# Reordering the first batch of a fused attention and maxout kernel: early scores, a weight transpose, and one load's place

## The chip, the cores and the metric

The kernel runs on one core of one Trainium2 chip. The metric is the device time of one execution in microseconds (us), lower is better. The core has a matrix engine (PE, with its weight loads as a row of their own, PEld), a vector engine (DVE), a scalar engine (ACT), GpSimd (POOL) and SyncE (SP), each with its own instruction stream, and 16 DMA engines that serve the loads and stores which SP, ACT and POOL issue.

## The reference

Block-causal attention over 8 batches, 8 heads, 576 tokens and head size 64 (blocks of 64 tokens), followed by a maxout layer on the 4608 tokens of width 512:

```python
scores = scale * np.matmul(q, k.transpose(0, 1, 3, 2))
mask = (pos // 64)[:, None] >= (pos // 64)[None, :]
scores = np.where(mask, scores, -1000000000.0)
attn = exp(scores - max) / (sum + 1e-09)
x = (attn @ v).transpose(0, 2, 1, 3).reshape(4608, 512)
h1 = x @ w1            # w1, w2: 512 x 1024
h2 = x @ w2
g = np.maximum(h1, h2)
return g @ w_out       # w_out: 1024 x 512
```

## The kernel before

The maxout is rewritten: max(h1, h2) = h2 + max(x (w1 - w2), 0). So the kernel forms `d_sb` = w1 - w2 (`diff_w`, DVE), the product `m_sb` = w2 w_out (from transposes of w2, `bT_unit`, and matmuls, `m_unit`), then for each span of tokens `g` = max(x d, 0) (`h_unit`) and the output rows y = x m + g w_out (`y_unit`). Inputs come as float32 and are cast to bf16; sums are float32.

Attention works on pairs of heads, p = 0 to 31, four pairs to a batch; two pairs are a group g, whose q and k come in one load each (`load_qk`, 576 KB, issued on SP). With `gated=True` POOL first writes one column of the load's tile with a memset (L119), and SP's issue waits for that memset; where the memset stands in POOL's stream is where the load is let go. `cast` makes bf16 of it (DVE, ACT or POOL), `transposes` turns it on PE into two PSUM tiles, whose copies to `qT` and `kT` are left to `copy_out`. V of a batch comes in five chunks (`load_v`, issued by POOL, which casts in flight). The weights are also loaded by POOL: w1 in `load_w`, w2 into a part of `xT` that is not in use yet, w_out in `load_wo`.

The scores of a pair are matmuls into one of two PSUM tiles (`ps_s`), exp on ACT writes them to `aT`, and small memsets (`mask`) clear what the block mask excludes. In batch 0 each pair has four bursts: `burst_p` covers the first 256 tokens, and `burst_q1`, `burst_q2`, `burst_q3` the rest. Later pairs have three tiles (`tile_0` to `tile_2`). `av(p, ts)` multiplies with V and scales by the sums on DVE; `x_out` transposes the result on PE and copies it to `xT`, in later batches a DMA does so.

Everything but the scores' tiles shares four rotating PSUM tiles (`ps_m`): a new one waits for the readers of the one four before it. For the transposes of group 1 in the first stage these are all four, and what comes next needs the copies of `cq` and `ck` in turn. `LOW` and `HIGH` split these copies by token, so that `burst_p` needs LOW alone.

The order of the first batch is written out by hand, line by line, and each engine takes its instructions in that order. `warm_up(n)` puts n matmuls of zeros (128x512) into PE's stream. `fill(n)` takes work worth n matmuls of 512 columns from a planned list of units (`h_unit`, `bT_unit`, `m_unit`, `y_unit`), first in the list whose tokens are there. A unit started is finished before the next. From the third group on a loop places scores, exps, products and fills; `pool_work(s)` there puts loads, casts and V chunks in POOL's stream, and is called by hand for s = 4 and s = 5.

The planned list starts with two h units, which need the first 256 tokens of x, then the transposes of w2's first piece, which need no token:

```python
for f in range(NFF):
    h(i, f)
    if i == 0 and f % 2:
        units.append((bT_unit(f // 2), 0, 0.25, 2 * NDM))
```

Of the kernel before, what the change touches and what calls it, by code (L numbers as in the profile page):

```python
# [14 lines left out]
def kernel(  # L15
# [10 lines left out]
    nc = tc.nc  # L26
# [33 lines left out]
    def a_col(p, c, t):  # L60
        if p >= HP:
            return CB[c] + t * P
        late = t * P >= QCUT
        return t * P + {
            0: 384 - QCUT if late else 0, 1: 704 - QCUT if late else 256 - P,
            2: 1024 - QCUT, 3: 1408 - 3 * P, 4: 1344 - 4 * P,
        }[c]
# [42 lines left out]
    dve, pool, act = nc.vector.tensor_copy, nc.gpsimd.tensor_copy, nc.scalar.copy  # L110

    def load_qk(g, queues, gated=False):
        b, u = divmod(g, GPB)
        for nm, src, queue in (("q", q, queues[0]), ("k", k, queues[1])):
            if queue is None:
                continue
            raws[nm, g] = t = raw.tile([P, 2, RPP * D], FP32, name=f"{nm}raw")
            if gated:
                nc.gpsimd.memset(t[:, 0, :1], 0.0)  # L119
            queue.dma_start(  # L120
                out=t[:],
                in_=src[b, 4 * u:4 * u + 4].rearrange(
                    "(s h) (p t) d -> (h p) s (t d)", h=2, t=RPP),
            )

    def cast(nm, g, parts):
        t = raws[nm, g].rearrange("p s (t d) -> p t s d", d=D)
        if (nm, g) not in qk_n:
            qk_n[nm, g] = qkn.tile([P, RPP, 2, D], BF16, name=f"{nm}n")
        n = qk_n[nm, g]  # L130
        for copy, j0, j1 in parts:
            copy(out=n[:, j0:j1], in_=t[:, j0:j1])  # L132

    def load_v(b, c):
        rows = min(P, S - c * P)
        nc.gpsimd.dma_start(  # L136
            out=vv_r[b % NV][P - rows:, c, :, :D],
            in_=v[b, :, c * P:c * P + rows, :].rearrange("h p d -> p h d"),
        )
# [20 lines left out]
    def diff_w(j):  # L160
        fs = slice(j * WB, (j + 1) * WB)
        nc.vector.tensor_sub(d_sb[:, :, fs], w1_raw[j][:], w2_sb[j])
# [8 lines left out]
    dve, pool, act = nc.vector.tensor_copy, nc.gpsimd.tensor_copy, nc.scalar.copy  # L171
    SP, ACT = nc.sync, nc.scalar
# [149 lines left out]
    def fill(n):  # L322
        while n > 0:
            if not current:
                k = next((k for k, t in enumerate(todo) if t[2] <= done_tokens[0]), None)
                if k is None:
                    return max(0, n)
                current.append(todo.pop(k))
            t = current[0]
            next(t[1])  # L330
            n -= t[3]
            t[0] -= 1
            if not t[0]:
                current.pop()
        return 0


    def warm_up(n):
        pw = ps_m.tile([P, SPAN], FP32, name="ps_w", tag="m")
        for _ in range(n):  # L340
            nc.tensor.matmul(pw[:], zeros[:, :P], zeros[:], start=True, stop=True)
# [57 lines left out]
    def mask(p, a0, eng=None):  # L399
        (eng or nc.gpsimd).memset(aT_r[p % NA][BLK:, :, a0:a0 + BLK], 0.0)  # L400

    def burst(p, parts, a0):
        u = ps_s.tile([P, 2, 512], FP32, name="ps_s", tag="s")
        w = 0
        for c, q0, n in parts:
            scores(p, u, w, c, q0, n)
            w += n
        exp(p, u, w, a0)

    def burst_p(p):  # L410
        burst(p, ((0, 0, QCUT), (1, P, QCUT - P)), 0)

    def burst_q1(p):
        burst(p, ((0, QCUT, 320), (1, QCUT, 192)), 384)

    def burst_q2(p):
        burst(p, ((1, 448, P), (2, QCUT, 320), (4, 512, BLK)), 896)

    def burst_q3(p):
        burst(p, ((3, 384, 192),), 1408)  # L420

    def masks_p(p, eng=None):
        for a in (0, 256):
            mask(p, a, eng)
# [7 lines left out]
    def tile_0(p):  # L432
        u = ps_s.tile([P, 2, 512], FP32, name="ps_s", tag="s")
        scores(p, u, 0, 0, 0, 512)
        return lambda: (exp(p, u, 512, 0), mask(p, 0))
# [27 lines left out]
    def av(p, ts):  # L463
        b, hp = divmod(p, HP)
        vv = vv_r[b % NV]
        a = aT_r[p % NA]
        n = len(ts)
        h0 = hp // 2 * 4 + hp % 2
        if p % 2 == 0 and ts[0] == 0:
            xps[p // 2] = xpool.tile([P, 2, NCH, 2, D], BF16, name="xp")  # L470
        xp = xps[p // 2]
        po = ps_m.tile([P, n, 2, D + 1], FP32, name="ps_o", tag="m")
        n_mm = 2 * sum(t + 1 for t in ts)
        mm = 0
        for gi, t in enumerate(ts):
            for hh in range(2):
                for c in range(t + 1):
                    a0 = a_col(p, c, t)
                    nc.tensor.matmul(  # L479
                        po[:, gi, hh, :], a[:, hh, a0:a0 + P], vv[:, c, h0 + 2 * hh, :],  # L480
                        start=(mm == 0), stop=(mm == n_mm - 1),
                    )
                    mm += 1
        rec = small.tile([P, 3, 2, 1], FP32, name="rec")
        nc.vector.reciprocal(rec[:, :n, :, 0], po[:, :, :, D])  # L485
        nc.vector.tensor_mul(  # L486
            xp[:, :, ts[0]:ts[0] + n, p % 2].rearrange("q s t d -> q t s d"), po[:, :, :, :D],
            rec[:, :n].to_broadcast([P, n, 2, D]),
        )

    def x_by_dma(g):
        return BY_DMA <= g < NG - 1
# [10 lines left out]
    def x_out(g, t0=0, t1=NCH, copies=(dve, dve)):  # L503
        b, u = divmod(g, GPB)
        if x_by_dma(g):
            if u == GPB - 1:
                done_tokens[0] = (b + 1) * S
            return
        xp = xps[g]
        n = t1 - t0  # L510
        n_odd = min(t1, NCH - 1) - t0
        pe = ps_m.tile([P, 2, n, BLK], BF16, name="ps_xe", tag="m")
        po = ps_m.tile([P, 2, n_odd, BLK], BF16, name="ps_xo", tag="m")
        for s in range(2):
            for t in range(t0, t1):
                src = xp[:, s, t].rearrange("p a d -> p (a d)")
                nc.tensor.transpose(pe[:, s, t - t0, :], src[:BLK], ident[:BLK, :BLK])
                if t < NCH - 1:
                    nc.tensor.transpose(po[:, s, t - t0, :], src[BLK:], ident[BLK:, BLK:])
        dst = xT[:, 2 * u:2 * u + 2, b * S + t0 * P:b * S + t1 * P].rearrange(  # L520
            "p s (t h w) -> p s t h w", h=2, w=BLK)
        copies[0](out=dst[:, :, :, 0], in_=pe[:])
        copies[1](out=dst[:, :, :n_odd, 1], in_=po[:])
        if u == GPB - 1:
            done_tokens[0] = min(b * S + t1 * P, (b + 1) * S)
# [14 lines left out]

    def pool_work(s):
        g, i = divmod(s, 2)
        if s == 4:
            load_qk(4, (SP, SP), gated=True)
        elif s == 5:
            load_qk(5, (SP, SP), gated=True)
            cast("q", 4, ((pool, 0, RPP),))
            cast("k", 4, ((pool, 0, RPP),))
        else:
            if i == 1 and g + 3 < NG:  # L550
                load_qk(g + 3, (SP, SP), gated=True)
            if i == 1 and g + 2 < NG:
                cast("q", g + 2, ((pool, 0, RPP),))
                cast("k", g + 2, ((pool, 0, RPP),))
            nb, j = divmod(s + 2, HP)
            if nb < B:
                for c in ((0, 1), (2, 3), (4,), ())[j]:
                    load_v(nb, c)
# [18 lines left out]
    HIGH = (LOW[1], NP)  # L577
    warm_up(16)
    cq = transposes("q", 0, (dve, act))
    ck = transposes("k", 0, (act, dve))  # L580
# [15 lines left out]
    cq = transposes("q", 1, (dve, dve))  # L596
    burst_q1(0)
    ck = transposes("k", 1, (dve, dve))
    for i in range(2):
        cq((i,), LOW)  # L600
        ck((i,), LOW)
    cq((0,), HIGH, act)
    cq((1,), HIGH, act)
    warm_up(3)
    burst_p(2)
    ck((0,), HIGH, dve)
    ck((1,), HIGH, dve)
    av(0, [0, 1])
    warm_up(2)
    burst_p(3)  # L610
    av(1, [0, 1])
    masks_p(2, nc.vector)
    burst_q3(0)
    masks_p(3, nc.vector)
    burst_q2(0)
    av(2, [0, 1])
    warm_up(2)
    x_out(0, 0, 2, (act, act))
    av(3, [0, 1])
    diff_w(0)  # L620
    burst_q1(1)
    warm_up(2)
    cast("q", 2, ((pool, 0, RPP),))
    masks_q(0)
    load_w(2)
# [25 lines left out]
    load_qk(3, (SP, SP), gated=True)  # L651
    for c in range(NCH):
        load_v(1, c)
    x_out(0, 2, NCH)
    diff_w(1)
    fill(2)
    outs = tile_0(4), tile_1(4)
    av(3, [2, 3, 4])
    region(*outs)
# [11 lines left out]
    n = fill_of(GPB)  # L671
    fill(n // 2)
    transposes("q", 3, (dve, act))()
    pool_work(4)
    fill(n // 3)
    transposes("k", 3, (dve, act))()
    pad_keys(6)
# [80 lines left out]
```

The softmax here doesn't subtract the row's maximum and nothing guards it: scores larger than these inputs give would overflow.

## Time and profile before

| what | value |
|---|---|
| median of 4 runs | 259.04 us (258.73 to 259.31) |
| the profiled execution | 259.31 us, span 257.5 us |
| PE busy | 244.7 us (95% of the span) |
| DVE, ACT, POOL busy | 136.0, 143.1, 110.1 us |
| DMA | 41.30 MB, mean 160 GB/s |
| q and k load, 576 KB each, median from issue to landing | 4.7 and 5.8 us |
| V chunk, 128 KB, the same | 5.4 us |

The span runs from the first to the last instruction of the profiled execution; the time also holds what lies around it. All times in the text count from the start of the span. A line of a timeline gives start, length, engine, source line, operation, tiles, shapes and count; in square brackets stands how long the engine was idle ahead of it, and what ended that. A line of the chain of waits gives start, length and what ran. A line of a DMA queue gives its packets, megabytes, and the time that its packets took as a share of 16 engines; packets overlap in an engine, so the share can exceed 100%.

### The profile page before, as it was taken

What the parts mean: (1) busy time and instruction counts of PE and PEld (TensorE: products, weight loads), DVE (VectorE), ACT (ScalarE), POOL (GpSimd) and SP (SyncE); (2) the same over time, 40 slices, a digit from 0 to 9 for tenths busy, and PEclk for the clock granted to TensorE, in tenths of its full rate; (3) what the DMA queues carried; (4) which work ended last, traced back from release to release, by engine and by line L of the source; (5) the groups of instructions that cost most, each with busy time, mean ns of one, the idle gap of its engine ahead of it and who ended that gap; (6) DMA issues with size and microseconds to landing.
All of it is one profiled execution on the core that took longest, in us unless ns stands there. A gap on an engine that the chain in (4) does not pass through costs nothing.

```text
span 257.5 us, 7161 instructions
## 1 busy us (share of the span) xinstructions
PE 244.7 (95%) x2949; PEld 139.3 (54%) x2983; DVE 136.0 (53%) x299; ACT 143.1 (56%) x200; POOL 110.1 (43%) x274
## 2 busy tenths in 40 slices
PE   8688999899999999999999999999999999999995
PEld 3346767756555555555555555555454555444444
DVE  5966986646684428442844284518451753443200
ACT  2788854567574857485748575866576421000111
POOL 2986950583637263726382637263813010000000
PEclk9999999999999999999999999999999999999999
DMA  7999999499579896997599959985975122202122
GB/s 251 310 222 302 208 256 240 161 139 223 151 148 264 137 221 104 249 150 238 92 258 138 194 134 233 162 209 127 87 115 100 45 63 73 83 0 81 43 105 99
DMA packets 71265, 41.30 MB, mean 160 GB/s; under 512 B 53568, under 2 KB 58048, under 8 KB 71232
## 3 DMA queue, kind: packets, MB, share of 16 engines
q1 hardware_dynamic: 28544, 31.27, 42.5%
q0 software_dynamic: 42272, 8.92, 38.8%
q10 hardware_dynamic: 416, 0.66, 0.7%
q8 instruction: 23, 0.38, 0.6%
q14 instruction: 10, 0.08, 0.1%
HBM read 34.60 MB, written 9.44 MB: 171 GB/s over the span
## 4 chain that ended last, share of the span: by engine, by line
PE 82%; DMA 10%; POOL 3%; issue 2%; ACT 1%; SPq 0%; DVE 0%; POOLq 0%; ACTq 0%
PE ps_y L257 36%; PE ps_h L215 22%; PE ps_o L479 10%; PE ps_s L371 7%; DMA qraw<-in_q_dram 5%; DMA kraw<-in_k_dram 3%; DMA vv<-in_v_dram 2%; PE ps_qT L352 2%; PE ps_kT L352 2%; PE ps_y L272 1%; PE ps_M L238 1%; POOL kn L132 1%; ACT aT L395 1%; PE ps_s L389 1%; POOL qn L132 1%
## 5 line engine op out<-in xcount | busy, mean ns | idle before, releaser
L395 ACT ACTIVATE aT<-ps_s 128x1024 bf16<-128x1024 f32 (+2 forms) x100 | 95.8, 996 | 26.2 <-PE ps_s L371 24.5
L257 PE MATMUL ps_y<-wo_sb,g 128*128 128x512 bf16 x275 | 69.1, 379 | 0.4 <-issue 0.3
L215 PE MATMUL ps_h<-xT,d_sb 128*128 128x512 bf16 (+3 forms) x306 | 67.4, 357 | 1.8 <-issue 1.0
L220 DVE TENSOR_SCALAR g<-ps_h 128x512 bf16<-128x512 f32 (+3 forms) x80 | 50.7, 636 | 30.6 <-PE ps_h L215 28.8
L400 POOL MEMSET aT<- 64x128 bf16 x124 | 22.3, 199 | 82.2 <-ACT aT L395 81.6
L485 DVE RECIPROCAL rec<-ps_o 128x4 f32<-128x4 f32 (+1 forms) x64 | 12.0, 188 | 62.9 <-PE ps_o L479 62.1
L215 PEld LDWEIGHTS <-d_sb 128*128 128x128 bf16 x320 | 29.0, 98 | 29.1 <-issue 2.7
L479 PEld LDWEIGHTS <-aT 128*128 128x128 bf16 x960 | 37.3, 98 | 13.8 <-issue 1.1
L262 ACT COPY y<-ps_y 128x512 f32<-128x512 f32 x31 | 18.2, 587 | 44.5 <-PE ps_y L257 32.6
L257 PEld LDWEIGHTS <-g 128*128 128x128 bf16 x280 | 25.8, 98 | 29.7 <-issue 2.0
L479 PE MATMUL ps_o<-vv,aT 128*128 128x65 bf16 x960 | 39.9, 194 | 0.2 <-DMA vv<-in_v_dram 0.2
L257 PE MATMUL ps_y<-m_sb,xT 128*128 128x512 bf16 x128 | 36.5, 380 | 1.2 <-issue 0.8
L136 POOL DMA_DIRECT2D vv<-in_v_dram x40 | 33.6, 847 | 1.6 <-issue 1.2
L371 PE MATMUL ps_s<-qT,kT 64*128 64x64 bf16 (+6 forms) x344 | 31.2, 280 | 1.9 <-ACT kT L360 0.7
L486 DVE TENSOR_TENSOR xp<-ps_o,rec 128x256 bf16<-128x256 f32 (+1 forms) x64 | 31.4, 491 | 2.2
L360 ACT COPY qT<-ps_qT 128x576 bf16<-128x576 bf16 (+1 forms) x17 | 10.3, 614 | 19.0 <-PE ps_qT L352 19.0
L257 PEld LDWEIGHTS <-xT 128*128 128x128 bf16 x140 | 12.2, 98 | 15.1 <-issue 3.5
L132 POOL CAST qn<-qraw 128x1152 bf16<-128x1152 f32 (+1 forms) x16 | 16.9, 1057 | 8.0 <-DMA qraw<-in_q_dram 8.0
L371 PEld LDWEIGHTS <-kT 64*128 64x128 bf16 x344 | 12.3, 94 | 11.0 <-issue 6.2
L360 ACT COPY kT<-ps_kT 128x576 bf16<-128x576 bf16 x15 | 9.6, 638 | 14.6 <-PE ps_kT L352 14.6
L132 POOL CAST kn<-kraw 128x1152 bf16<-128x1152 f32 (+1 forms) x15 | 17.1, 1137 | 1.4 <-DMA kraw<-in_k_dram 1.3
L207 POOL COPY g<-g 128x512 bf16<-128x512 bf16 x8 | 4.9, 611 | 20.7 <-DVE g L220 20.3
(58 smaller groups left out, 161.8 us busy)
## 6 DMA issues: line engine op xcount, KB each, us to landing
qraw<-in_q_dram SPq DMA_DIRECT2D x16, 576.0 KB, 4.7
out_dram<-y SPq DMA_DIRECT2D x35, 256.0 KB, 3.5
kraw<-in_k_dram SPq DMA_DIRECT2D x15, 576.0 KB, 5.8
vv<-in_v_dram POOLq DMA_DIRECT2D x32, 128.0 KB, 5.4
w1raw<-in_moe_w_dram POOLq DMA_DIRECT2D x4, 512.0 KB, 8.5
xT<-in_moe_w_dram POOLq DMA_DIRECT2D x4, 256.0 KB, 8.9
wo_sb<-in_moe_w_out_dram POOLq DMA_DIRECT2D x2, 512.0 KB, 10.3
kraw<-in_k_dram ACTq DMA_DIRECT2D x1, 576.0 KB, 5.3
```

The costliest lines, as they stand in the source:

```text
L132: copy(out=n[:, j0:j1], in_=t[:, j0:j1])
L136: nc.gpsimd.dma_start(out=vv_r[b % NV][P - rows:, c, :, :D], in_=v[b, :, c * P:c * P + rows, :].rearrange("h p d -> p h d"),)
L215: nc.tensor.matmul(pt[:, :w], d_sb[:, c, f * P:(f + 1) * P], xT[:, c, t0:t0 + w], start=(c == 0), stop=(c == NDM - 1),)
L220: nc.vector.tensor_scalar_max(g[:, f, m:m + w], pt[:, :w], 0.0)
L257: nc.tensor.matmul(py[:], lhs, rhs, start=(n == 0), stop=(n == len(terms) - 1),)
L262: (dve if i < 2 else act)(out=y[:], in_=py[:])
L360: (copy or copies[i])(out=t[:, p0 * RPP:p1 * RPP].rearrange("q (p j) -> q p j", j=RPP), in_=pts[i][:, :, p0:p1].rearrange("q j p -> q p j"),)
L371: nc.tensor.matmul(ps[:, hh, col:col + w], kT[r, k0:k0 + P], qT[r, q0:q0 + w], start=True, stop=True,)
L395: nc.scalar.activation(out=aT_r[p % NA][:, :, a0:a0 + w], in_=ps[:, :, :w], func=AF.Exp, scale=scale,)
L400: (eng or nc.gpsimd).memset(aT_r[p % NA][BLK:, :, a0:a0 + BLK], 0.0)
L479: nc.tensor.matmul(po[:, gi, hh, :], a[:, hh, a0:a0 + P], vv[:, c, h0 + 2 * hh, :], start=(mm == 0), stop=(mm == n_mm - 1),)
L486: nc.vector.tensor_mul(xp[:, :, ts[0]:ts[0] + n, p % 2].rearrange("q s t d -> q t s d"), po[:, :, :, :D], rec[:, :n].to_broadcast([P, n, 2 ...
```

## The change

Five edits in the first stages, with the same arithmetic:

1. `burst_p(2)` and `burst_p(3)` follow one another, with no zeros between, right after the first copies of group 1. The masks of these pairs and the HIGH copies of q come between them on DVE.
2. The two HIGH copies of q, and the first two copies of `x_out(0, 0, 2)`, go from ACT to DVE.
3. `av(0)` and `av(1)` stand together, ahead of `burst_q3(0)`; nine zero matmuls of this stretch become two.
4. A `fill(2)` stands where the last of those zeros stood. No token of x is ready there, so it takes the eight transposes of w2's first piece; the `fill(2)` ahead of `tile_0(4)` that took them goes.
5. The load of the fifth group (g = 4) is let go directly behind the five V chunks of batch 1, in place of behind the casts of group 3.

```diff
     def pool_work(s):
         g, i = divmod(s, 2)
-        if s == 4:
-            load_qk(4, (SP, SP), gated=True)
-        elif s == 5:
+        if s == 5:
             load_qk(5, (SP, SP), gated=True)
...
-    cq((0,), HIGH, act)
-    cq((1,), HIGH, act)
-    warm_up(3)
+    cq((0,), HIGH)
     burst_p(2)
-    ck((0,), HIGH, dve)
-    ck((1,), HIGH, dve)
+    masks_p(2, nc.vector)
+    burst_p(3)
+    cq((1,), HIGH)
+    masks_p(3, nc.vector)
+    ck((0,), HIGH)
+    ck((1,), HIGH)
     av(0, [0, 1])
+    av(1, [0, 1])
+    burst_q3(0)
     warm_up(2)
-    burst_p(3)
-    av(1, [0, 1])
-    masks_p(2, nc.vector)
-    burst_q3(0)
-    masks_p(3, nc.vector)
     burst_q2(0)
     av(2, [0, 1])
-    warm_up(2)
-    x_out(0, 0, 2, (act, act))
+    x_out(0, 0, 2)
     av(3, [0, 1])
     diff_w(0)
     burst_q1(1)
-    warm_up(2)
+    fill(2)
     cast("q", 2, ((pool, 0, RPP),))
...
     load_qk(3, (SP, SP), gated=True)
     for c in range(NCH):
         load_v(1, c)
+    load_qk(4, (SP, SP), gated=True)
     x_out(0, 2, NCH)
     diff_w(1)
-    fill(2)
     outs = tile_0(4), tile_1(4)
...
     fill(n // 2)
     transposes("q", 3, (dve, act))()
-    pool_work(4)
     fill(n // 3)
```

## The prediction

> **What bounds the kernel now.** I read the page's busy shares first, then the table by stage, then the chain of waits in order of time, then the timelines of single engines and the DMA packets in single microseconds.
>
> ```profile
> PE 244.7 (95%) x2949; PEld 139.3 (54%) x2983; DVE 136.0 (53%) x299; ACT 143.1 (56%) x200; POOL 110.1 (43%) x274
> ```
> ```profile
> 12.00:18.00 6.00, 5.26 (x74) 2.47 (x74) 3.91 (x15) 4.54 (x8) 5.60 (x10) 1.00 1.68 201
> 25.00:34.00 9.00, 7.92 (x134) 6.03 (x127) 8.86 (x19) 7.88 (x11) 7.97 (x19) 1.00 1.34 239
> 34.00:46.00 12.00, 11.95 (x155) 9.13 (x152) 8.24 (x19) 4.83 (x7) 3.82 (x11) 1.00 1.63 249
> 46.00:60.00 14.00, 13.09 (x215) 8.54 (x218) 8.08 (x20) 8.71 (x12) 9.79 (x22) 1.00 0.72 153
> ```
>
> Columns: window, length, busy time of PE, PE's weight loads, DVE, ACT, POOL, then clock, DMA share, GB/s. PE is the bound from 34 us to the end; before 34 it shares the bound with DVE and ACT. So time gained or lost ahead of 34 us, and every hole of PE after it, goes into the end one for one. The chain of waits shows the one large hole that the change can reach, ahead of the q transposes of group 4 at 46.70 us:
>
> ```profile
> 28.52 8.80 DMA kraw<-in_k_dram
> 37.33 0.05 issue
> 37.38 1.15 POOL kn L132
> ...
> 38.59 6.78 DMA qraw<-in_q_dram
> ...
> 45.50 1.15 POOL qn L132
> 46.65 0.05 issue
> 46.70 0.44 PE ps_qT L352 x18
> ```
> ```profile
> 46.70 0.44 PE L352 MATMUL ps_qT<-ident,qn 64*128 64x64 bf16 x18 [0.74 <-POOL qn L132]
> ```
>
> The fifth load (group 4) is issued at 38.59 because its gate stands on POOL behind the casts of group 3, which wait for their own load. It lands at 45.4, and PE idles 0.74 us. The second place is the start:
>
> ```profile
> 11.91 0.81 PE L341 MATMUL ps_w<-zeros 128*128 128x512 bf16 x3 [1.17 <-ACT qT L360]
> ...
> 18.80 1.11 PE L215 MATMUL ps_h<-xT,d_sb 128*128 128x256 bf16 x8
> ```
>
> **What the Trainium skill says.** "DMA: Bandwidth & Descriptors", section Queues, rings and completion order: each DMA engine takes turns between the queues that have work, a packet from each. The trace agrees. From 33 to 34 us, with q and k of group 3 on q1 and weights and V on q0, both move the same number of packets; from 37 to 38, with q1 empty, V on q0 moves ten times as many:
>
> ```profile
> q1 hardware_dynamic: 125, 0.28, 81.1%
> q0 software_dynamic: 123, 0.04, 36.4%
> ```
> ```profile
> q0 software_dynamic: 1192, 0.16, 239.3%
> ```
>
> So V, in small packets, nearly stops while q and k move. The same page, section Anatomy of one DMA, puts a fixed 2 us on a DMA, most of it between last byte and signal: V's last packets move from 42 to 43 us and its last chunk lands at 44.3, so 1.3 us or more here. "TensorE: Matmul & The Clock Gate", section Part 1, says that the array falls to half clock after about 3.4 us of idleness; nothing before shows that happening after the start, as the longest hole past 2 us is 1.17 us.
>
> **The change part by part.**
>
> *Zeros.* Seven fewer 128x512 zero matmuls: at 0.27 us (two take 0.54 us of issue at 17.10) 1.9 us of PE work. None of it is saved directly, since PE waits for other engines there.
>
> *Pairs 3 and 4 back to back.* burst_p(2) now waits only for the first column parts on DVE (11.21 us), so its scores go at 11.28 instead of 12.65, those of pair 4 at 11.93 instead of 13.97. The exps end at 12.47 and 13.21, 1.4 and 2.0 us earlier. But av(0) still waits for the second V chunk, landed at 13.31, so PE gains nothing there; ACT idles instead.
>
> *Work moved to DVE.* From ACT: two 315-wide copies (0.40 each of issue) and two x copies (0.2 to 0.28 each). From later: the first w2 copy, 0.68 (0.60 of issue). DVE is in order, and its masks now wait for the exps at 12.47 and 13.21. My chain on DVE: q part 11.80 to 12.25; masks of pair 3 12.52; q part 12.70 to 13.12; masks of pair 4 13.26; two k parts to 14.27; av(0), av(1) (0.56 each) to 15.42; av(2) to 16.0; x copies to 16.35; av(3) to 16.9. diff_w(0) then waits for w2's first piece (issue 10.03 + 7.1 = 17.13), the same for the transposes on PE; it runs 17.18 to 18.40, the w2 copy to 18.99, the second x copies to 19.39. Before they ended at 19.05. The third matmul of the first h unit needs them: PE is **0.34 late**, and so is the exp chain from 20.29 on, through masks on POOL and the cast of k2 to the k transposes (24.67, now 25.0).
>
> *w2 transposes moved.* At 25.87 PE loses 0.24 of idle and 0.6 of work, DVE 0.68 of copy. tile_0(4) needs the k copy (25.92 + 0.34 = 26.26), so it goes at 26.3 instead of 26.41. But diff_w(1) ends at 27.87 on DVE (27.52 before), so h follows at 27.95 (27.70), the ACT copy of the second w2 piece at 29.47 (29.22), the exps behind it and the scores at 32.55 that wait for them by the same 0.25. At 34 us I take **+0.25**. Bounds -0.5 (all of the 0.85 at 25.87 gained, less the 0.34) and +0.7 (nothing of it).
>
> *Fifth q, k behind V.* Two small memsets (0.1 each) move on POOL to behind the five V issues that end at 32.09; ahead of masks, so those lose under 0.1. SP is idle there (it waits for POOL gates), so its two issues go at about 32.6 instead of 38.6, on q1 directly behind group 3. Group 3 finishes its packets at 36.2 and group 4 follows; it lands before 42.5, when its casts can start (behind pad_keys, 41.87, and the gate of group 5, 42.34). The hole goes: **-0.74**.
>
> The price is V of batch 1. Group 3 took 544 packets; at the 129 per us of q1 from 33 to 36, group 4 takes 4.1 us, to 40.3. In that time V gets 530 packets instead of some 4000. What is left of its 4430 after 36 us, 3900 at 1200 per us, takes 3.25 us: the bulk ends at 43.6, not 39.85. Before, the last chunk landed 4.45 us behind the bulk (44.3), because group 4 came in at 39.8 and cut into V's tail. Now group 5, gated at 42.34 and some 1.2 us from issue to packets, comes in at about 43.6, the same place. With the same tail V lands at 48.0; with none, at 43.6 + 1.4 = 45.0. PE wants chunk 4 in av(4) at 45.6 + 0.25 = 45.85. So the stall lies between 0 and 2.2 us; I take **+1.4**. All PE work of the q transposes stands behind it in order. No gain later pays it back, as PE is the bound.
>
> Sum: 0.25 - 0.74 + 1.4 = +0.9. The profiled execution took 259.31 us (span 257.5), so it would be 260.2; it lies 0.27 above the median of the runs, 259.04, so the forecast is **259.9**.
>
> **The rivals.**
>
> *V in time* (not slower). V's packets were all queued before group 4's, and if the engines serve V first, or its tail is short, no stall comes: 0.25 - 0.74 = -0.5, 258.5, and -1.2 with the best front. For it: V began at full rate when group 3 ended, and k of group 2, issued at 14.0 behind V, moved only from 16.5. Against it: the equal packet counts at 33 us, and q of group 3 landed (35.2) ahead of weights issued 2.5 us before it (38.0).
>
> *No earlier landing.* If group 4 waits behind V altogether, it moves from 40 us as before; the hole stays in part: +0.25 - 0 to 0.74, about 259.0.
>
> *The clock falls* (slower). Without zeros PE does 0.7 us of work from 10.74 to 13.36 us. If that counts as idle, some 3.5 us of array work up to 18 us doubles, part of it beside waits: +1 to +2.5, 260 to 261.5. Against it: the longest full hole stays near 1.1 us. It decides from a whole window of idleness.
>
> **How the numbers follow.** V late 0.58, V in time 0.27, no earlier landing 0.08, clock 0.07. About 0.2%, 0.52 us, is what a measurement can tell from no change. V late gives +0.3 to +1.7: 0.49 slower, 0.09 same. V in time: 0.18 faster, 0.09 same. No earlier landing: 0.02 and 0.06. Clock: 0.06 slower, 0.01 same. Together faster 0.20, same 0.25, slower 0.55. The likeliest case alone spans 259.3 to 260.7; the range reaches down to the middle of V in time, with part of its best front, and up to a full stall with front +0.4: 258.3 to 261.3.
>
> **What would show it.** Right: a PE wait of about a microsecond for DMA vv in av(4) near 46 us, no wait for POOL at the q transposes behind it, V's packets at some 130 per us from 36 to 40 us, and the first h unit near 19.1 to 19.4. Wrong: V landing by 45.5, 1200 packets per us from 36 us on; matmuls of 128x512 above 0.5 us near 15 us (the clock); or PE reaching 34 us over half a microsecond earlier.

## The result, and the profile after

The changed kernel takes 259.80 us, median of 36 runs (259.11 to 261.96), against 259.01 us (57 runs of the kernel before beside them): ratio 1.0034, 95% interval 1.0022 to 1.0046. It is slower by 0.8 us. The forecast was 259.9. The ratio is the recorded one, not the quotient of the two medians (1.0031 here); in the experiments the two differ by up to 0.0015, which is 0.4 us, so where it matters both are given.

The profiled execution of the changed kernel took 261.13 us (span 259.4), the second-slowest of 37 with it, for two reasons that must be taken off before it is set against the profile of before: its first 16 zero matmuls took 6.41 us against 5.69 (other runs of either order show 5.1 to 6.4), so everything behind them starts 0.7 us later; and the clock of PE fell. It shows where time can go, not how much goes in a usual run. The profiled run of the kernel before (259.31) is not a usual one either: 13 of the 57 runs took longer. Busy shares and the clock's row, from the page of the changed kernel:

```profile
PE 246.3 (95%) x2942; PEld 140.3 (54%) x2976; DVE 137.2 (53%) x303; ACT 142.1 (55%) x196; POOL 110.1 (42%) x274
...
PEclk9959999999999999999999999999999999999999
```

PE has seven instructions fewer, yet is busy 1.6 us longer, all of it ahead of the q transposes of group 4 (41.5 us busy up to there, 40.0 before). The first zeros have 0.72 of it. The clock is the sixth value after the length in the table by stage, counts in brackets aside:

```profile
12.00:18.00 6.00, 4.66 (x54) 2.46 (x56) 4.91 (x20) 3.27 (x5) 5.02 (x10) 0.64 1.62 203
18.00:25.00 7.00, 6.42 (x117) 4.77 (x117) 5.22 (x12) 5.29 (x7) 3.54 (x7) 0.82 1.21 311
25.00:34.00 9.00, 7.81 (x150) 5.68 (x147) 7.85 (x17) 7.90 (x11) 8.67 (x15) 1.00 1.16 169
34.00:46.00 12.00, 11.61 (x135) 8.72 (x135) 8.51 (x19) 6.04 (x9) 6.08 (x19) 1.00 1.53 263
```

In the kernel before, the second of these stages was:

```profile
18.00:25.00 7.00, 6.37 (x154) 4.76 (x147) 4.67 (x12) 6.15 (x9) 4.60 (x10) 1.00 1.23 312
```

From 12 to 18 us PE does 54 matmuls where it did 74 (seven zeros and the later start are in that too), at a mean clock of 0.64. PE's timeline from 11.9 us:

```profile
11.96 0.34 PE L371 MATMUL ps_s<-qT,kT 64*128 64x256 bf16 x4 [0.53 <-DVE kT L360]
12.63 0.34 PE L371 MATMUL ps_s<-qT,kT 64*128 64x256 bf16 x4 [0.33 <-DVE kT L360]
...
13.96 0.49 PE L479 MATMUL ps_o<-vv,aT 128*128 128x65 bf16 x6 [0.60 <-DVE qT L360]
...
14.72 0.59 PE L341 MATMUL ps_w<-zeros 128*128 128x512 bf16 x1
...
17.96 1.04 PE L227 MATMUL ps_bT<-ident,xT 128*128 128x128 bf16 x8
...
20.83 1.05 PE L215 MATMUL ps_h<-xT,d_sb 128*128 128x256 bf16 x8
```

The two bursts of scores go back to back, as the edit says. A single zero matmul of 512 columns takes 0.59 us, where another one of this profile, at 9.82 us and full clock, takes 0.39: the array is at half clock (0.50 from 14 us on). That is one of the signs which the prediction named for being wrong. The first h unit, forecast for 19.1 to 19.4, starts at 20.83. At the place of the fifth load's casts, the same timeline:

```profile
46.90 0.44 PE L479 MATMUL ps_o<-vv,aT 128*128 128x65 bf16 x9
47.69 0.76 PE L479 MATMUL ps_o<-vv,aT 128*128 128x65 bf16 x15 [0.35 <-DMA vv<-in_v_dram]
48.38 0.44 PE L352 MATMUL ps_qT<-ident,qn 64*128 64x64 bf16 x18
```

The wait for POOL ahead of the q transposes is gone; a shorter wait for V stands in av(4). From these q transposes to the end of the span it is 211.0 us here (259.4 less 48.38) and 210.8 before (257.5 less 46.70), and 210.8 to 211.0 in the profile of every experiment. So all that differs between these profiles is made ahead of this point.

The chain of waits of the changed kernel shows what this V chunk has become, a transfer of 15 us:

```profile
30.74 1.73 POOL vv L136 x2
32.47 15.18 DMA vv<-in_v_dram
47.65 0.04 issue
47.69 0.76 PE ps_o L479 x15
```

The five V chunks of this batch take 13.4 to 15.2 us from issue to landing, where they took 11.3 to 13.3 before, so the change adds some 2 us to each. SP's timeline has the fifth load at 34.19 instead of 38.59; the forecast had 32.6, but POOL comes to the gate later in this profile (in experiment 1 the load goes at 32.12):

```profile
34.19 0.37 SPq L120 DMA_DIRECT2D qraw<-in_q_dram  x1
34.66 0.41 SPq L120 DMA_DIRECT2D kraw<-in_k_dram  x1
```

And the DMA queues of the changed kernel, first from 40 to 41 us, then from 43 to 44, with q and k on q1 and V on q0:

```profile
q1 hardware_dynamic: 150, 0.31, 91.5%
q0 software_dynamic: 146, 0.02, 28.3%
```
```profile
q0 software_dynamic: 1216, 0.15, 240.8%
```

V is held to the packet rate of q and k, and gets 1216 per us only when group 4 is through, at 42 us.

### The profile page after: what moved, and what is told of

It reads as the page before. It is cut to its first block, busy times and chain, and to the rows that moved or that the text cites. A ratio compares the mean times of both kernels' runs of the same rounds, so it can differ in the third digit from the quotient of the medians.

```text
span 259.4 us, 7149 instructions
## 1 busy us (share of the span) xinstructions
PE 246.3 (95%) x2942; PEld 140.3 (54%) x2976; DVE 137.2 (53%) x303; ACT 142.1 (55%) x196; POOL 110.1 (42%) x274
## 4 chain that ended last, share of the span: by engine, by line
PE 85%; DMA 6%; POOL 3%; issue 2%; ACT 2%; DVE 1%; ACTq 0%; POOLq 0%
PE ps_y L257 35%; PE ps_h L215 21%; PE ps_o L479 10%; PE ps_s L371 8%; DMA vv<-in_v_dram 6%; PE ps_w L341 3%; PE ps_qT L352 2%; PE ps_kT L352 2%; ACT aT L395 1%; PE ps_y L272 1%; POOL vv L136 1%; PE ps_M L238 1%; PE ps_s L389 1%; POOL wo_sb L168 1%; PE ps_xe L517 1%
## 5 line engine op out<-in xcount | busy, mean ns | idle before, releaser
L262 ACT COPY y<-ps_y 128x512 f32<-128x512 f32 x31 | 18.2, 587 | 44.8 <-PE ps_y L257 32.6
L479 PE MATMUL ps_o<-vv,aT 128*128 128x65 bf16 x960 | 40.5, 194 | 1.0 <-DVE qT L360 0.6
L371 PE MATMUL ps_s<-qT,kT 64*128 64x64 bf16 (+6 forms) x344 | 32.0, 285 | 3.1 <-DVE kT L360 1.2
L360 ACT COPY qT<-ps_qT 128x576 bf16<-128x576 bf16 x15 | 9.6, 638 | 18.6 <-PE ps_qT L352 18.6
```

The costliest lines, as they stand in the source:

```text
L262: (dve if i < 2 else act)(out=y[:], in_=py[:])
L360: (copy or copies[i])(out=t[:, p0 * RPP:p1 * RPP].rearrange("q (p j) -> q p j", j=RPP), in_=pts[i][:, :, p0:p1].rearrange("q j p -> q p j"),)
L371: nc.tensor.matmul(ps[:, hh, col:col + w], kT[r, k0:k0 + P], qT[r, q0:q0 + w], start=True, stop=True,)
L479: nc.tensor.matmul(po[:, gi, hh, :], a[:, hh, a0:a0 + P], vv[:, c, h0 + 2 * hh, :], start=(mm == 0), stop=(mm == n_mm - 1),)
```

## The experiments

Each ratio is to the kernel before on the same chip. Two theories were set against each other: **V late**, as forecast (the load of group 4 takes V's turns, and PE waits for V), and **front**, in which the loss comes from the reordered first 34 us or from the clock.

**1. The load alone.** The kernel before, with only the fifth load moved:

```diff
     for c in range(NCH):
         load_v(1, c)
+    load_qk(4, (SP, SP), gated=True)
...
-    pool_work(4)
```

> The kernel before with the fifth load alone moved behind V of batch 1. Theory A (the forecast: V of batch 1 comes late and that is the loss): the POOL wait of 0.74 us ahead of the q transposes near 46 us is gone, a wait for DMA vv of about 1.4 us stands in av(4), together +0.7 us on the kernel before. Theory B (the front is the loss, the load is not): a wait for vv of 0.35 us or less, as in the changed kernel's profile, and -0.4 us or lower. V moves at about 130 packets per us while group 4 is on its way in both.

259.96 us (before 258.62), ratio 1.0056 (1.0043 to 1.0068). PE's timeline:

```profile
44.94 0.64 PE L479 MATMUL ps_o<-vv,aT 128*128 128x65 bf16 x9
46.56 0.84 PE L479 MATMUL ps_o<-vv,aT 128*128 128x65 bf16 x15 [0.98 <-DMA vv<-in_v_dram]
47.33 0.44 PE L352 MATMUL ps_qT<-ident,qn 64*128 64x64 bf16 x18
```

From the first of these lines to the q transposes 2.39 us pass. Where nothing is waited for, the same 24 matmuls take 0.82 us up to the q transposes (45.36 to 46.18 in experiment 10 below), so 1.57 us are lost to V in this profile. The hole ahead of the q transposes is gone. Here are the DMA queues of this experiment from 38 to 39 us, with both moving the same:

```profile
q1 hardware_dynamic: 146, 0.31, 89.7%
q0 software_dynamic: 148, 0.02, 31.2%
```

V runs freely from 40 us on: 948 packets from 40 to 41 us, 918 from 42 to 43 and 316 from 43 to 44, so its bulk ends near 43. V late is thus shown as a mechanism. By itself it costs more than the whole change (five runs; the two intervals just overlap).

**2. The front alone.** The changed kernel with the load put back to `pool_work(4)`:

> The changed kernel with the fifth load put back to where it was before. Theory A (the forecast): +0.25 us on the kernel before, from DVE, with the POOL wait of 0.74 us back. Theory B (the front is the loss): +1.0 us or more, with PE at half clock for some microseconds between 13 and 21 us in several of the runs and the first h unit a microsecond or more later than 18.80.

259.18 us, ratio 1.0036 (1.0019 to 1.0054). In 8 of 14 runs the clock held (mean clock of the run above 0.995): median 258.91, 0.3 us above before. In the other 6 it fell: median 260.47. Over all runs that is 0.56 us by the medians, 0.93 by the ratio. So the front has a cost of its own, and in nearly half of the runs it is not the one that was forecast.

**3 and 4. Parts of the front.** Experiment 3 takes the w2 transposes early (edit 4 alone), experiment 4 moves the copies to DVE (edit 2 alone):

```diff
-    warm_up(2)
+    fill(2)
     cast("q", 2, ((pool, 0, RPP),))
...
-    fill(2)
     outs = tile_0(4), tile_1(4)
```

> The kernel before with the first w2 transposes alone moved into batch 0, in place of two zero matmuls. By the forecast's DVE chain the copy (0.60 of issue) stands ahead of the second x copies, which had 0.47 us of slack behind them only on DVE, none on PE: the first h unit 0.5 us later, then 0.85 us of PE and 0.6 us of DVE gained near 26 us: between -0.3 and +0.3 us in all. If the front's loss is the w2 copy on DVE: +0.5 us or more. No fall of the clock, as five zero matmuls stay ahead of it.

```diff
-    cq((0,), HIGH, act)
-    cq((1,), HIGH, act)
+    cq((0,), HIGH)
+    cq((1,), HIGH)
...
-    x_out(0, 0, 2, (act, act))
+    x_out(0, 0, 2)
```

> The kernel before with the four copies alone moved from ACT to DVE (two HIGH copies of q, two x copies). By the forecast's rows DVE gets 1.2 us more ahead of 19 us, of which its 1.9 us of idle there take most: 0 to +0.4 us. If the front's loss is mainly DVE: +0.7 us or more. No fall of the clock, as all zeros stay.

Measured 259.14 (1.0018, 1.0007 to 1.0030) and 259.23 (1.0029, 1.0016 to 1.0042), before 258.62. By the ratios they cost about 0.5 and 0.75 us. In PE's timeline of experiment 3 the h unit waits where the forecast said, at its third matmul, for the x copies behind the w2 copy on DVE:

```profile
19.15 0.39 PE L215 MATMUL ps_h<-xT,d_sb 128*128 128x256 bf16 x2
20.03 0.81 PE L215 MATMUL ps_h<-xT,d_sb 128*128 128x256 bf16 x6 [0.49 <-DVE xT L523]
```

In experiment 4 the copies in front of the three zeros take DVE's time instead of ACT's, and PE waits 1.58 us for `qT` where it waited 1.17. In both profiles the wait for POOL at 46.7 us has vanished: a PE that comes later finds the casts of group 4 done. The hole of the kernel before thus covers up to 0.74 us of delay in the front. Where the runs lose their half microsecond the two profiles do not show: PE reaches the q transposes at 46.69 and 46.42 us, no later than in the profile of before, whose run was itself 0.7 us above the median of this batch.

**5 and 6. Group 5 out of V's way.** In `pool_work(5)` the casts of group 4 go ahead of the gate of group 5, which moves that load from about 43 to 45 us; once on experiment 1, once on the changed kernel:

```diff
         if s == 5:
-            load_qk(5, (SP, SP), gated=True)
             cast("q", 4, ((pool, 0, RPP),))
             cast("k", 4, ((pool, 0, RPP),))
+            load_qk(5, (SP, SP), gated=True)
```

> The kernel of e1 (only the fifth load moved), with the gate of the sixth load (group 5) moved on POOL from ahead of the casts of group 4 to behind them, some 2.3 us later. Theory A (V late because q and k take turns with it, and its tail stretched because group 5 comes in at its end): V's bulk still ends near 43.2 us, but the tail has the engines to itself, the last chunk lands near 45 us, the wait for vv in av(4) shrinks from 1.0 us to under 0.3: 0 to -0.7 us on the kernel before, 1.4 us or more under e1. Rival (V's tail is long by itself, from engines that are behind): the wait stays at 1 us and the time at +1 us or more.

> The changed kernel with the gate of group 5 behind the casts of group 4. Theory A: no wait for vv, no POOL wait at 46 us: front of +0.3 and hole of -0.74 left, -0.3 to 0 us on the kernel before in runs without a fall of the clock, +1 us in those with a long one. Rival (V is no part of the changed kernel's loss, the front is all): as the changed kernel, +0.8 us.

On experiment 1: 259.34 us (before 258.99), 1.0013 (0.9988 to 1.0037). On the changed kernel: 259.56, 1.0015 (0.9992 to 1.0037). Both are below their starting points (1.0056 and 1.0034), the second with overlapping intervals. But experiment 5's profile, one of its slower runs (260.79), still waits for V, with q1 empty from 43 to 45 us. Its DMA queues from 43 to 44 us and from 44 to 45, and then those of the kernel before from 40 to 41, where group 4 moves beside V's tail:

```profile
q0 software_dynamic: 153, 0.02, 129.0%
```
```profile
q0 software_dynamic: 166, 0.02, 57.8%
```
```profile
q0 software_dynamic: 151, 0.02, 137.1%
q1 hardware_dynamic: 54, 0.12, 61.9%
```

In the first two there is no line for q1. V's last packets come as slowly without any rival as beside one. The forecast had put the whole length of the tail down to the load that comes in at its end; that holds for a part of it at most. Experiment 6's profile (259.26, one of its faster runs) has no wait for V that stands out:

```profile
45.47 1.14 PE L479 MATMUL ps_o<-vv,aT 128*128 128x65 bf16 x24
46.55 0.44 PE L352 MATMUL ps_qT<-ident,qn 64*128 64x64 bf16 x18
```

Its 24 matmuls take 1.08 us up to the q transposes, 0.26 more than the least. So the tail is not equally long in the two profiles, though both let group 5 go late.

**7. Zeros put back into the changed kernel**, inside the score tiles, so that they need no PSUM tile of their own:

```diff
-    burst_p(2)
+    burst_p(2, 2)
...
-    burst_p(3)
+    burst_p(3, 2)
...
-    burst_q3(0)
-    warm_up(2)
+    burst_q3(0, 2)
+    warm_up(3)
```

The second argument is the number of 128x512 zero matmuls ahead of the scores.

> The changed kernel with seven zero matmuls back: two each in the score tiles of pairs 3 and 4 and of burst_q3(0), ahead of the scores, and one more behind it. If the fall of the clock comes from the missing zeros, no run falls under 0.99 and the slowest runs (above 260.6 us) are gone, with the median 0.1 to 0.4 us lower than the changed kernel's: +0.5 us on the kernel before. If the zeros do nothing against it, falls in a third or more of the runs, as in the changed kernel.

The clock fell in 1 of 22 runs, so the zeros hold it. But the time is 260.15 us, 1.0045 (1.0027 to 1.0062), not below the changed kernel. PE's timeline of experiment 7 says why:

```profile
45.33 0.53 PE L481 MATMUL ps_o<-vv,aT 128*128 128x65 bf16 x9
46.91 0.86 PE L481 MATMUL ps_o<-vv,aT 128*128 128x65 bf16 x15 [1.06 <-DMA vv<-in_v_dram]
47.71 0.44 PE L352 MATMUL ps_qT<-ident,qn 64*128 64x64 bf16 x18
```

PE comes to av(4) earlier and waits longer: V lands near 47 us all the same. By the measure of experiment 1 it loses 1.56 us to V (45.33 to 47.71, less 0.82), where the changed kernel's profile loses 0.66 (46.90 to 48.38, less 0.82). The expectation of a lower median failed, and so did that of no slow runs: four of the 22 are above 260.6 us.

**8. Seven zeros out of the kernel before**: all three `warm_up` ahead of `x_out(0, 0, 2)` removed.

> The kernel before without seven of its zero matmuls (three ahead of burst_p(2), two behind av(0), two ahead of x_out). If these zeros hold the clock: half clock for 3 to 7 us between 12 and 21 us in several runs, those 1 us or more slower. If not: 0 to -0.3 us, as 1.9 us of PE work goes that lies beside waits.

259.08 us, 0.9989 (0.9969 to 1.0009). The clock fell in 6 of 14 runs (median 259.31; 258.78 where it held). With experiment 7 this shows that it is the zeros that hold the clock, in either order.

**9 and 10. Only q of group 4 early.** q goes behind the V chunks, k is let go with group 5's gate; on the kernel before and on the changed one:

```diff
         if s == 5:
+            load_qk(4, (None, SP), gated=True)
             load_qk(5, (SP, SP), gated=True)
...
         load_v(1, c)
+    load_qk(4, (SP, None), gated=True)
```

> The kernel before with q of group 4 alone moved behind V of batch 1, and k of group 4 let go later, with group 5's gate near 42.3 us. Theory A (q and k take turns with V, so V is late by the packets that go ahead of it): V gives way for 2.05 us, not 4.1, its bulk ends near 41.7 us instead of 43.2, the last chunk lands by 45 us, no wait for vv in av(4) and no POOL wait at 46 us: -0.5 to -0.7 us on the kernel before. Rival (V's tail on the engines that are behind is the whole lateness, whatever goes ahead): a wait for vv of 0.5 us or more, +0.3 us or more.

> The changed kernel with the same split of group 4's q and k. Theory A: no wait for vv; the front's +0.3 us and the gain of 0.74 us remain, so -0.4 us on the kernel before where the clock holds, +1 us where it falls long; median -0.2 us. Rival (the front is the loss): +0.8 us as in the changed kernel.

On the kernel before: 258.33 us (before 258.71), 0.9981 (0.9966 to 0.9995), the only version that beats both kernels with its whole interval, the kernel before only just. In its DMA queues from 38 to 39 us V already runs at full rate:

```profile
q0 software_dynamic: 1045, 0.14, 209.0%
q1 hardware_dynamic: 23, 0.04, 11.6%
```

PE still waits 0.63 us for V in its profile, a sign that the expectation gave to its rival; but the profiled run, at 259.27 us, is one of the slowest of the 22. On the changed kernel: 258.91 us, 0.9999 (0.9986 to 1.0012), with no wait for V and none for POOL in PE's timeline:

```profile
45.36 0.89 PE L479 MATMUL ps_o<-vv,aT 128*128 128x65 bf16 x24
46.18 0.44 PE L352 MATMUL ps_qT<-ident,qn 64*128 64x64 bf16 x18
```

Letting k go late again takes 0.35% off the changed kernel by the ratios, about 0.9 us, which is the whole of its loss; by the medians (0.80 and 0.20 us above before) it is 0.6, most of it. The clock fell in 10 of these 22 runs, and their median is 258.96 against 258.88 for the others. It held in the profiled one, and there the first h unit waits at its third matmul, as forecast, for the x copies on DVE:

```profile
19.52 0.81 PE L215 MATMUL ps_h<-xT,d_sb 128*128 128x256 bf16 x6 [0.60 <-DVE xT L523]
```

**11 and 12. Two attempts to find a gain in the order.** Experiment 11 is experiment 9 with `warm_up(3)` and `burst_p(2)` made one tile, `burst_p(2, 3)`. Experiment 12 is the changed kernel's order alone, with load, w2 transposes and copies as before:

> The kernel of e9, and the three zeros ahead of burst_p(2) put into its own score tile, so that they don't wait for a copy of q on ACT (1.17 us of PE idle at 11.91): scores of pair 3 at 11.7 instead of 12.65 us. Theory A: with V no longer late a faster front shows in the time: -0.7 to -1.2 us on the kernel before. If it is V that sets the time still: as e9.

> The kernel before with the change's order of scores, masks and av in batch 0 and five zero matmuls fewer; the copies stay on ACT, the w2 transposes and the load stay where they were. If the loss of the front is DVE's added copies (e3, e4): -0.3 to +0.2 us where the clock holds. If it is the order itself (masks on DVE that wait for the exps): +0.5 us or more. Falls of the clock in a quarter of the runs or more, these 0.5 to 1.5 us slower.

Experiment 11: 258.74 us, 0.9993 (0.9974 to 1.0012). The 0.7 to 1.2 us expected are not there in the median; it can't be told from experiment 9. But its runs fall into two halves: 11 of 22 lie between 257.90 and 258.52 us, eight of them below all 75 runs of the kernel before, and 11 lie from 258.96 up. The clock fell in three of the upper half, too few to explain it; the profiled run (257.98) is of the lower half, so no trace shows what holds the others back.

Experiment 12: 259.34 us, 1.0025 (1.0006 to 1.0045), clock fallen in 14 of 22 runs. The fall does not explain the loss: the median is 259.33 us with it, 259.58 in the eight runs without. The profiled run kept its clock. Its first h unit starts at 18.25 us, earlier than the 18.80 of before, but then PE waits for V of batch 0, and later the hole is back:

```profile
22.04 0.34 PE L479 MATMUL ps_o<-vv,aT 128*128 128x65 bf16 x6 [1.21 <-DMA vv<-in_v_dram]
...
47.21 0.44 PE L352 MATMUL ps_qT<-ident,qn 64*128 64x64 bf16 x18 [0.83 <-POOL qn L132]
```

So in this profile the order without its zeros gains half a microsecond ahead of 19 us and loses more in the next wait. In the median it brings nothing; whether the other runs wait for the same chunk is not shown.

## Why the prediction was right, point by point

- **V late: right in its mechanism.** Equal packet counts on both queues, the bulk's end (near 43 us in experiment 1, worked out as 43.6), the wait in av(4) and all work behind it: each is in a trace. That the queues take turns packet by packet ("DMA: Bandwidth & Descriptors" in the Trainium skill, section Queues, rings and completion order) holds here too, 150 to 146 from 40 to 41 us.
- **V's size, +1.4: right with the clock held, wrong in the changed kernel's own profile.** The loss to V is 1.57 us in the profile of experiment 1 and 1.56 in that of experiment 7, but 0.66 in the changed kernel's. The step that failed there is the pair of landing and wanted time: 45.85 us was taken for the latter. In experiment 7 PE does stand idle from 45.85 (46.91 less 1.06). In the changed kernel's profile it does so only from 47.34 (47.69 less 0.35), 1.5 us later, of which the start has 0.7; V lands at 47.65, against some 46.5 in experiment 1. The front delayed PE by more than it delayed V. (The chunk waited for is the fourth of five, as nine matmuls are done; the forecast had the last.) In the runs, V is worth 0.6 to 0.9 us within the change (the changed kernel against experiment 10); alone it is worth the 1.3 to 1.45 of experiment 1 and what the hole gave back, at most 0.74.
- **V's tail.** "Group 4 came in at 39.8 and cut into V's tail" is only part of the cause: experiment 5's tail is as slow with q1 empty.
- **The hole, -0.74: right that it goes.** It is gone in the changed kernel and in the profiles of experiments 1, 5 to 7, 9 and 10. Its size comes from one profile and is not steady: profiles with the load at its old place have 0.83 (experiment 12), 0.34 (experiment 8) and 0.17 (experiment 2). Experiment 9, which takes it away, gained 0.4 us.
- **The front, +0.25: right only where the clock holds.** The scores of pairs 3 and 4 go at 11.96 and 12.63, less the later start 11.26 and 11.93; worked out were 11.28 and 11.93. Experiment 2 has +0.3 in runs that keep the clock, but +0.56 (medians) to +0.93 (ratio) over all its runs. The step that failed is the argument against the clock, that the longest full hole stays near 1.1 us. Nothing in the changed kernel stands still that long behind the start, and the clock fell in 17 of 37 runs. A chance of 0.07 was far too low for that. Edit by edit, the w2 transposes and the copies cost more in the runs than was worked out, half a microsecond and more; and the wait of av(1) for the HIGH copy of q (0.60 us), behind the masks on DVE, was not foreseen.
- **Why the clock moved the median so little.** Runs of the changed kernel with the clock held have a median of 259.75 us, with it fallen 260.03. Two depths show. Where the mean clock of the run is 0.991 to 0.993 (13 runs), their median is 259.80, about as with the clock held; where it is 0.985 to 0.987 (4 runs) they lie at 260.42 to 261.96. Experiment 7 held the clock and gained nothing, as V was then waited for longer.
- **The sum was right by offset, and so in part by luck.** Worked out: 0.25 - 0.74 + 1.4 = +0.9. Two profiles come to nearly this sum in two ways. In experiment 7, which keeps its clock, PE reaches av(4) 0.27 us later than before (45.33 against 45.06), and V in place of the hole adds 0.74: +1.0, as forecast part by part. In the changed kernel's profile PE reaches av(4) 1.84 us later (46.90), of which the start has 0.7 and the front with its clock 1.1, and V in place of the hole takes 0.16 back: again +1.0 without the start. By the runs: the front with its clock +0.6 to +0.9 (experiment 2), and the load on top of it -0.05 (ratios) to +0.2 (medians). The parts don't add up freely: the front's delay eats into the wait for V, and in the kernel before it eats into the hole.

What stays open: why some runs of one kernel lose the clock and others don't; what makes V's last packets slow with q1 empty; where experiments 3 and 4 lose their half microsecond; and what splits the runs of experiment 11.

## What to carry to other kernels

A load that was issued earlier took turns here from a transfer that was already under way, so ask which of the two is wanted first, and in which part (here q early and k late gained 0.4 us, both early lost 1.3). Zero matmuls between real ones may look like waste on an engine that waits anyway; the longest hole did not tell here that the clock would fall, nor did the busy share, so read the clock of many runs before taking zeros out. Price two edits together when both end in the same wait: a delay ahead of it is free until the wait is used up.

## What the runs showed of the hardware

- The array's clock fell without a long hole. In the changed kernel's profile PE was busy in parts from 10 to 14 us, 0.38 to 0.68 of each microsecond, with no hole above 0.60 us, and the clock was 0.50 from 14 us. The kernel before has a hole of 1.17 us at 11 us, zeros right behind it, and keeps its clock. "TensorE: Matmul & The Clock Gate" in the Trainium skill, section Part 1: The HAM clock gate, has the fall after an idle window of about 3.4 us; here no such window was idle, and the measurement decides. Nor does the busy share alone tell: experiment 10's profile has 0.79, 0.47, 0.63 and 0.41 in the same four microseconds and keeps its clock.
- The half clock lasted some 6.8 us in this profile (13.7 to 20.6, worked out from the mean clock of windows of 1 and 3 us) and 3.4 in experiment 6's (14.5 to 17.9). Half of 6.8 us in a span of 259 is 0.013, half of 3.4 is 0.007: the two depths of 0.987 and 0.993 in the list of runs. One or two windows of the length that the section names fit both.
- How often the clock fell, by kernel: with all zeros in place (before, in three batches) 0 of 37, 1 of 51 and 0 of 75 runs; experiments 1, 4, 5 and 9, 0 of 5, 1 of 19, 1 of 14 and 0 of 22; zeros put back (experiment 7) 1 of 22; two zeros fewer (experiment 3) 0 of 11; five or seven fewer (the changed kernel, experiments 2, 6, 8, 10 and 12) 17 of 37, 6 of 14, 5 of 14, 6 of 14, 10 of 22 and 14 of 22. In experiment 11, where three zeros stand earlier, it fell in 3 of 22.
- V's small packets (some 120 bytes: 0.15 MB in 1216) fall from some 1200 to 150 per us, an eighth, while q and k in packets of about 2 KB (0.31 MB in 150) pass. And with q1 empty from 43 to 45 us in experiment 5, V's last packets came at 153 and 166 per us, about the rate that they had beside q1 in the kernel before (151 from 40 to 41 us).
